# Two token tiles of a gated block computed from centred tokens, with the scale moved into the gelu

## The chip, the cores and the metric

The kernel runs on one core of a Trainium2 chip. The metric is the device time of one execution in microseconds (us); three runs of the kernel before gave a median of 200.08 us. The profile is of one further execution of 199.44 us, whose span from first to last instruction is 197.7 us.

The engines, as the profile names them: PE does the matrix products (PEld is its weight load, which runs beside the products), DVE and ACT do elementwise work, POOL does small work and issues some transfers, and SP only issues transfers. A core has 16 DMA engines that all queues share.

## The reference

`x` is 2048 tokens of 512 channels in bf16. The output is `x + A(xn) + B(xn)`, with `xn` the layer norm of `x`:

```python
def _layernorm(x, axis=-1, eps=1e-05):
    m = mean(x); v = var(x)
    return (x - m) / jnp.sqrt(v + eps)

# A: attention of 32 heads of 16; each query sees 8 keys, 2 apart
qkv = xn @ wqkv
logits = einsum('bhsd,bhswd->bhsw', q, k[idx]) * scale    # idx = pos - {0,2,..,14}
o = einsum('bhsw,bhswd->bhsd', softmax(logits), v[idx])
a = o @ wo

# B: a gated block, F = 1376, half of it 688
z  = gelu(xn @ w_in)
z1 = z[..., :688]
z2 = layernorm(z[..., 688:])
g  = einsum('ts,bsf->btf', w_sp, z2) + b_sp      # mixes all 2048 tokens
b  = (z1 * g) @ w_out

out = x + a + b
```

The norm is a mean to subtract and one factor per token to multiply by. The product with `w_in` is linear in the token, so the factor can be applied before it or after it.

## The kernel before, in words

The tokens are 16 tiles of 128. The program is a set of named steps. Five lists, one for each engine, hold the order in which the engines issue the steps; nothing reorders them, and an instruction that must wait holds all that stands behind it on its engine. The names that matter here, with i the tile:

- `x` loads tokens (tiles 0 to 3 alone, then 4-5, 6-7, 8-11 and 12-15 together) through SP's queue. The same queue carries the weights: `wz0`, `wz1`, `wz2` (the z2 half of `w_in` in three pieces), `wy` (its z1 half), `wk`, `wq`, `wv`.
- `b{i}` and `ag{i}` on DVE make mean and variance of a token (L172 and L178). `gr{i}` on POOL makes the factor: an add of eps (L182; for tiles 0 and 1 an `ep{i}` on DVE, L200, does that) and a power of -1/2 (L183). `n{i}` on DVE writes the normed tile (L186; tile 0 in two halves, L190).
- PE's products need the normed tile turned, with channels on the partitions, in the tile `xnT`. Tiles 0 to 3 are turned by PE itself: `T{i}` is four transposes into PSUM (L225), and `Tc{i}` on ACT copies them to `xnT` (L228; tiles 0, 1 and 2 in two halves). Tiles 4 to 15 are turned by DMA: `t{i}` is a transpose that SP issues (L208). The profile calls the memory of tokens and normed tiles `z`.
- `z{i}` is the z2 half of `xn @ w_in` for a tile: 8 products of 128x344 (L247). Tile 0's are `z0a` and `z0b`; those of tiles 1 and 2 are cut into `Z{i}` (the first few) and `z{i}` (the rest). `h{i}` on ACT is its gelu (L264). `y{i}` and `yg{i}` are the same for the z1 half (L247 and L339).
- `k`, `q`, `v` are the heads (L350), each copied out by ACT (`kc`, `qc`, `vc`, L363). They read `xnT` of all tiles.
- `m`, `f`, `p` on DVE and POOL make the attention logits from q and k in eight units of a quarter of the head's channels and a half of the tokens: `m` multiplies (L393), `f` folds two halves into one by an accumulating DMA that POOL issues (L401; only the first unit's fold is on DVE), `p` sums (L406). `kh` are small copies of k's edges; POOL issues `kh2` and `kh3`.
- `M{j}` mixes all tokens with `w_sp` (L512), and the end of the program multiplies by `wo` and `w_out` (L566, L573, L580), adds and stores.

`wu` is ten products on constants at the very start (L496), and `wd` three more; both only keep PE busy. Three PSUM tiles `mm` go round among z, y, k, q, v and M, two tiles `aux` among the `T`.

The order on PE is `wu T0a T0 B wd z0a T1 z0b Z1 T2 z1 Z2 T3 z2 z3 y0 y1 y2 y3 z4 ... z14`, then the heads, then `z15 y4 ... y15`, `M0 ... M15` and the end.

## Time and profile before

| | before |
|---|---|
| median of three runs | 200.08 us (199.61 to 200.2) |
| the profiled execution | 199.44 us |
| its span | 197.7 us |
| PE busy | 192.8 us, 98% of the span |
| DVE busy | 179.2 us, 91% |
| ACT busy | 87.9 us, 44% |
| POOL busy | 43.4 us, 22% |

A row of a timeline holds the start in us from the span's start, how long the row lasted, the engine (SPq is SP's queue), the line, the operation, out<-in, the shape and how many instructions it merges; in square brackets stand the engine's idle time before it and what ended that. In the view of one line's instructions stand shortest/median/longest in ns, then first and last start in us, and below that the time from a DMA's issue to its landing. A row of the view by stretches holds for each engine its busy time and instruction count, then the granted clock of PE (1.00 is full), the busy share of the DMA engines (it passes 1 when transfers of several queues overlap on an engine) and GB/s. A row of a DMA queue holds packets, MB and the time of the packets as a share of 16 engines over the stretch asked for.

### The profile page before, as it was taken

How to read it: one execution, taken by the hardware profiler on the slowest of the kernel's cores; microseconds unless marked ns; L12 is line 12 of the kernel's file. 1: busy time of each engine (PE TensorE's matmuls, PEld its weight loads, DVE VectorE, ACT ScalarE, POOL GpSimd, SP SyncE). 2: the span in 40 equal slices, each digit the busy share in tenths (PEclk: the TensorE clock that was granted, in tenths of full speed). 3: DMA queues.
4: the chain of work that ended last, by engine and by line, in shares of the span. 5: the costliest groups of instructions: out<-in, count | busy, mean ns of one | idle time of the engine just before them, and what ended most of it. 6: DMA issues, size and time to landing. Idle time of an engine off the chain costs nothing.

```text
span 197.7 us, 4588 instructions
## 1 busy us (share of the span) xinstructions
PE 192.8 (98%) x1944; PEld 121.5 (61%) x1944; DVE 179.2 (91%) x214; ACT 87.9 (44%) x128; POOL 43.4 (22%) x79
## 2 busy tenths in 40 slices
PE   7899999999999999999999999999999999999993
PEld 2466666666666666666666666666666654444442
DVE  4899896799989999999999999999999999999073
ACT  2476798785558967792562311112221110044000
POOL 4477322001565326355000000011120000000000
PEclk9999999999999999999999999999999999999999
DMA  4999552499999999989699999999979227402433
GB/s 148 354 338 133 90 107 83 71 154 135 254 206 211 202 185 146 190 177 185 128 209 252 186 217 276 162 242 266 213 154 241 54 48 219 86 2 83 136 106 106
DMA packets 71252, 33.40 MB, mean 169 GB/s; under 512 B 59488, under 2 KB 69248, under 8 KB 71104
## 3 DMA queue, kind: packets, MB, share of 16 engines
q1 hardware_dynamic: 68400, 25.38, 61.6%
q0 software_dynamic: 2688, 7.70, 20.0%
q8 instruction: 15, 0.25, 0.5%
q10 hardware_dynamic: 144, 0.03, 0.1%
q14 instruction: 5, 0.04, 0.1%
HBM read 10.13 MB, written 2.10 MB: 62 GB/s over the span
## 4 chain that ended last, share of the span: by engine, by line
PE 93%; DMA 2%; SPq 1%; DVE 1%; issue 1%; DVEq 0%
PE mm L512 38%; PE mm L350 21%; PE mm L247 18%; PE mm L580 7%; PE mm L566 6%; PE aux L566 2%; DMA z<-in_A_x_dram 2%; PE mm L573 1%; SPq L255 1%; SPq L165 1%; PE aux L225 0%; DVE stats L172 0%; DVE z L628 0%; DVE z L186 0%; PE aux L580 0%
## 5 line engine op out<-in xcount | busy, mean ns | idle before, releaser
L512 PE MATMUL mm<-z,wsp 128*128 128x344 bf16 x512 | 74.8, 309 | 0.0
L512 PEld LDWEIGHTS <-wsp 128*128 128x128 bf16 x512 | 50.1, 98 | 24.6
L350 PE MATMUL mm<-xnT,wts 128*32 128x512 bf16 x768 | 41.7, 379 | 0.0
L247 PE MATMUL mm<-wts,xnT 128*128 128x344 bf16 x256 | 38.3, 309 | 0.0
L350 PEld LDWEIGHTS <-wts 128*32 128x32 bf16 x768 | 28.7, 139 | 12.8 <-issue 0.3
L460 DVE TENSOR_TENSOR prod<-vp,a_sb 128x4096 bf16<-128x4096 bf16 x16 | 36.2, 2282 | 0.0
L247 PEld LDWEIGHTS <-xnT 128*128 128x128 bf16 x256 | 24.6, 98 | 12.5 <-ACT xnT L228 0.6
L528 ACT ACTIVATE qk<-mm,b_col 128x688 bf16<-128x688 f32 x16 | 13.3, 830 | 42.4 <-PE mm L512 40.2
L393 DVE TENSOR_TENSOR prod<-qk 128x4096 bf16<-128x4096 bf16 (+1 forms) x15 | 27.2, 1860 | 1.2 <-ACT qk L363 1.1
L464 DVE TENSOR_TENSOR prod<-prod,prod 128x8192 bf16<-128x8192 bf16 (+1 forms) x7 | 26.7, 3809 | 0.1
L363 ACT CAST qk<-mm 128x1024 bf16<-128x1024 f32 x16 | 16.2, 1012 | 8.2 <-PE mm L350 8.2
L580 PE MATMUL mm<-wts,xnT 32*128 32x512 bf16 x192 | 14.5, 374 | 0.0
L523 POOL DMA_DIRECT2D qk<-qk x8 | 3.9, 497 | 47.9 <-DMA qk<-z 40.3
L339 ACT ACTIVATE z<-mm 128x688 bf16<-128x688 f32 x16 | 11.8, 742 | 4.2 <-PE mm L247 3.4
L264 ACT ACTIVATE z<-mm 128x688 bf16<-128x688 f32 x16 | 11.8, 744 | 3.2 <-PE mm L247 3.2
L566 PEld LDWEIGHTS <-qk 128*128 128x128 bf16 x75 | 7.3, 98 | 8.9 <-issue 0.4
L566 PE MATMUL mm<-wts,qk 128*128 128x512 bf16 x55 | 12.4, 379 | 0.0
L172 DVE BATCH_NORM_STATS2 stats<-z 128x6 f32<-128x512 bf16 x15 | 10.1, 673 | 2.0 <-DMA z<-in_A_x_dram 1.9
L401 POOL DMA_DIRECT2D prod<-prod x10 | 8.8, 978 | 11.6 <-DVE prod L393 11.6
L580 PEld LDWEIGHTS <-xnT 32*128 32x128 bf16 x256 | 6.7, 93 | 7.2
L183 POOL TENSOR_TENSOR rstd<-rstd,mhalf 128x1 f32<-128x1 f32 x16 | 9.0, 562 | 3.7 <-DVE rstd L200 2.6
L616 ACT CAST z<-mm 128x512 bf16<-128x512 f32 x6 | 3.3, 600 | 13.6 <-PE mm L580 13.6
(93 smaller groups left out, 179.0 us busy)
## 6 DMA issues: line engine op xcount, KB each, us to landing
prod<-prod POOLq DMA_DIRECT2D x10, 512.0 KB, 7.9
wts<-in_A_wo_dram SPq DMA_DIRECT2D x4, 512.0 KB, 6.7
wsp<-in_A_x_dram SPq DMA_DIRECT2D x2, 1024.0 KB, 6.5
out_dram<-z SPq DMA_DIRECT2D x15, 128.0 KB, 1.8
wts<-in_A_wqkv_dram SPq DMA_DIRECT2D x3, 512.0 KB, 6.4
z<-in_A_x_dram SPq DMA_DIRECT2D x2, 512.0 KB, 7.6
wsp<-z POOLq DMA_DIRECT2D x2, 512.0 KB, 8.8
wsp<-wts POOLq DMA_DIRECT2D x2, 512.0 KB, 8.4
```

The costliest lines, as they stand in the source:

```text
L247: PE.matmul(t[:, hh, 0:FHALF], xnT[:, kc, i * P:(i + 1) * P], w_z[part][:, kc, hh * FHALF:(hh + 1) * FHALF], start=(kc == 0), stop=(kc == ...
L264: A.activation(z2[:, i, :].rearrange("p (a b) -> p a b", a=2), t[:, :, 0:FHALF], ACT.Gelu_apprx_tanh, **total)
L339: op_(f"yg{i}", [f"y{i}"] + ["p10"] * (i >= 10), lambda: A.activation(z1u[:, i, 0:FH].rearrange("p (a b) -> p a b", a=2), t[:, :, 0:FHALF] ...
L350: PE.matmul(t[32 * g:32 * g + 32, dd, :], w, r, start=(kc == 0), stop=(kc == C - 1), tile_position=(0, 32 * g))
L363: op_(f"{a}c{p}", [f"{a}{p}"], lambda: A.copy(home(a, p), t[:].rearrange("p d (t s) -> p d t s", t=2)))
L393: V.tensor_tensor(pr[:, w0:w1], q[:, w0:w1], k[:, w0:w1], ALU.mult)
L460: return lambda: V.tensor_tensor(dst, vp[:, :, th, off:off + GS], a_sb[:, th, W - 1 - w].unsqueeze(1).broadcast_to([P, DH, GS]), ALU.mult)
L464: return lambda: V.tensor_tensor(dst, dst, x, ALU.add)
L512: PE.matmul(t[:, hh, 0:FHALF], w[:, k, (j % 2) * P:(j % 2 + 1) * P], z2[:, k, hh * FHALF:(hh + 1) * FHALF], start=(k == 0), stop=(k == NT ...
L528: lambda: A.activation(gs[j % 3].rearrange("p (a b) -> p a b", a=2), t[:, :, 0:FHALF], ACT.Identity, bias=b_col[:, j:j + 1]))
L566: PE.matmul(po[i][:, c], uT[th][:, m, t0:t0 + P], wout[:, m, c], start=(start and m == 0), stop=(stop and m == MF - 1))
L580: PE.matmul(po[groups[n][g]], op[32 * g:32 * g + 32, th, d, s * P:(s + 1) * P], wo_r[32 * g:32 * g + 32, d, :], start=False, stop=(d == DH ...
```

## The change

Four things are changed.

1. **Tiles 0 and 1 are centred, not normed, for z and y.** ACT makes minus the centred tile 0 in two halves (`c0a`, `c0b`, L197), as soon as the mean is there; DVE makes the same of tile 1 (`c1`, L201). PE turns these into `xcT`, a part of the `z2` memory that is free until late in z. The factor is made for both tiles at once on POOL (`gr0`), negated there (`nr`, L202), and taken by the four gelus of these tiles as a scale for each token. The normed tiles 0 and 1 are still made (`n0`, `n1`), since the heads read them; they are now turned by two more DMA transposes, `t0` and `t1`, which SP issues behind `wk` and ahead of `t4`.
2. **The order at the start.** DVE's statistics of tile 2 are one instruction instead of two; eps is added on DVE for tiles 2 and 3 instead of 0 and 1; `n3` stands ahead of `b4`; `wu` has 8 products instead of 10; `B` (which turns the bias) stands behind `T1`; `Z1` and `Z2` have six products each instead of four and two; ACT does `h0` ahead of tile 2's copies.
3. **`y4` and its gelu `yg4` move** from behind the heads to a place right behind `y3`, ahead of `z4`.
4. **`f01`**, the fold of the second unit, moves ahead of `kh2` in POOL's list.

```diff
-    stats2 = sb.tile([P, 2, 6], F32, name="stats2")
+    nrstd = sb.tile([P, 2], F32, name="nrstd")
...
+    xc = [z2_r[:, 13 * FH + n * D:13 * FH + (n + 1) * D] for n in range(2)]
+    xcT = z2_r[:, 13 * FH + 2 * D:13 * FH + 4 * D].rearrange("p (c s) -> p c s", c=C)
...
+    def gscale(i):
+        return {"scale": nrstd[:, i:i + 1]} if i < 2 else {}
...
+    def center_half(n):
         c = slice(n * D // 2, (n + 1) * D // 2)
-        V.tensor_scalar(xn[0][:, c], xs[:, 0, c], mv[:, 0, 0:1], rstd[:, 0:1], ALU.subtract, ALU.mult)
+        A.activation(xc[0][:, c], xs[:, 0, c], ACT.Identity, bias=mv[:, 0, 0:1], scale=-1.0)
+
+    op_("c0a", ["ag0"], lambda: center_half(0))
+    op_("c0b", ["c0a"], lambda: center_half(1))
+    op_("c1", ["ag1"], lambda: V.tensor_scalar(xc[1], xs[:, 1, :], mv[:, 1, 0:1], -1.0, ALU.subtract, ALU.mult))
+    op_("nr", ["gr0"], lambda: G.tensor_scalar(nrstd[:], rstd[:, 0:2], -1.0, 1.0, ALU.mult, ALU.mult))
...
-        if i >= NPE:
+        if tok(i)[1] != "c":
             op_(f"t{i}", [f"n{i}"], lambda i=i: SP.dma_start_transpose(xnT[:, :, i * P:(i + 1) * P], xn[i % 8]))
...
+    def turned_of(i):
+        return xcT[:, :, i * P:(i + 1) * P] if i < 2 else xnT[:, :, i * P:(i + 1) * P]
...
-            PE.matmul(t[:, hh, 0:FHALF], xnT[:, kc, i * P:(i + 1) * P], w_z[part][:, kc, hh * FHALF:(hh + 1) * FHALF],
+            PE.matmul(t[:, hh, 0:FHALF], turned_of(i)[:, kc], w_z[part][:, kc, hh * FHALF:(hh + 1) * FHALF],
                       start=(kc == 0), stop=(kc == C - 1))
...
-    SPLIT = {1: 4, 2: 2}
+    SPLIT = {1: 6, 2: 6}
...
-    op_("wu", [], lambda: spin(aux[1], D, 10))
+    op_("wu", [], lambda: spin(aux[1], D, 8))
...
-    pe = """wu T0a T0 B wd z0a T1 z0b Z1 T2 z1 Z2 T3 z2 z3 y0 y1 y2 y3 z4 z5 z6 z7 z8 z9 z10 z11 z12 z13 z14
+    pe = """wu T0a T0 wd z0a T1 B z0b Z1 T2 z1 Z2 T3 z2 z3 y0 y1 y2 y3 y4 z4 z5 z6 z7 z8 z9 z10 z11 z12 z13 z14
...
-    dve = """b0 ag0 ep0 b1 n0a ag1 ep1 n0 b2a n1 b2 ag2 b3 ag3 n2 b4 ag4 n3 b5 ag5 n4 b6 ag6 n5 b7""".split()
+    dve = """b0 ag0 b1 ag1 c1 b2 ag2 ep2 n0 n2 b3 ag3 ep3 n1 n3 b4 ag4 b5 ag5 n4 b6 ag6 n5 b7""".split()
...
-    pool = ["b16"] + [f"gr{i}" for i in range(NT)] + "zr0 zr4 kh2 f01 f10 zr8 f11 kh3 f20 f21 zr12 f30 f31 LO5 V00 V01 V02 V03".split()
-    sp = """x0 x1 x2 wz0 wz1 wz2 x3 x4 x6 wy x8 x12 wk t4 t5 t6 t7 t8 t9 t10 t11 t12 t13 t14 t15 wq kh0a kh0b W0 kh1 wv W1 vh
+    pool = ["b16"] + ["gr0", "nr"] + [f"gr{i}" for i in range(2, NT)] + "zr0 zr4 f01 kh2 f10 zr8 f11 kh3 f20 f21 zr12 f30 f31 LO5 V00 V01 V02 V03".split()
+    sp = """x0 x1 x2 wz0 wz1 wz2 x3 x4 x6 wy x8 x12 wk t0 t1 t4 t5 t6 t7 t8 t9 t10 t11 t12 t13 t14 t15 wq kh0a kh0b W0 kh1 wv W1 vh
```

How the instructions stand: first SP's queue, where the token loads, `wk` and the transposes of tokens meet. Before:

```order
L259 DMA wts<-in_B_w_in_dram 128x4x688
L165 DMA z_88<-in_A_x_dram 128x4x512 x2
L256 DMA wts<-in_A_wqkv_dram 128x4x512
L208 DMA_TRANSPOSE xnT<-z_88 128x4x128 x12
L257 DMA wts<-in_A_wqkv_dram 128x4x512
```

And now (all lines are about 8 further down in the changed file):

```order
L267 DMA wts<-in_B_w_in_dram 128x4x688
L174 DMA z_88<-in_A_x_dram 128x4x512 x2
L264 DMA wts<-in_A_wqkv_dram 128x4x512
L213 DMA_TRANSPOSE xnT<-z_88 128x4x128 x14
L265 DMA wts<-in_A_wqkv_dram 128x4x512
```

There are 14 transposes instead of 12; the first two are `t0` and `t1`, and `t4` is now the third behind `wk`.

Second, ACT from its start to the gelu of tile 3 (`mm_92` to `mm_94` are the three PSUM tiles of z, `aux_95` and `aux_96` those of the turns). Before:

```order
L659 ACT_TABLE_LOAD
L228 COPY xnT<-aux_95 128x2x128 [waits PE_49]
L228 COPY xnT<-aux_96 128x2x128 [waits PE_49]
L506 CAST b_col<-mm_94 128x16 [waits PE_49]
L228 COPY xnT<-aux_95 128x2x128 [waits PE_49]
L228 COPY xnT<-aux_95 128x2x128
L228 COPY xnT<-aux_96 128x2x128 [waits PE_49]
L228 COPY xnT<-aux_96 128x2x128
L264 ACTIVATE z_86<-mm_92 128x688
L228 COPY xnT<-aux_95 128x4x128 [waits PE_49]
L264 ACTIVATE z_86<-mm_93 128x688
```

And now:

```order
L667 ACT_TABLE_LOAD
L197 ACTIVATE z_86<-z_88,mv 128x256 [waits DMAHW0_49,DVE_49]
L197 ACTIVATE z_86<-z_88,mv 128x256
L236 COPY z_86<-aux_95 128x2x128 [waits PE_49]
L236 COPY z_86<-aux_96 128x2x128 [waits PE_49]
L236 COPY z_86<-aux_95 128x2x128 [waits PE_49]
L236 COPY z_86<-aux_95 128x2x128
L514 CAST b_col<-mm_94 128x16 [waits PE_49]
L272 ACTIVATE z_86<-mm_92,nrstd 128x688 [waits PE_49,Pool_49]
L236 COPY xnT<-aux_96 128x2x128 [waits PE_49]
L236 COPY xnT<-aux_96 128x2x128
L272 ACTIVATE z_86<-mm_93,nrstd 128x688 [waits PE_49]
```

Two activations stand ahead of the first copy, and tile 0's gelu now stands ahead of tile 2's copies and takes `nrstd`, which comes from POOL.

Third, PE at the end of `y3` and the first products of the next tile, which before is `z4`:

```order
L247 LDWEIGHTS xnT
L247 MATMUL mm_93<-wts,xnT 128x344
L247 LDWEIGHTS xnT [waits DMAHW5_49]
L247 MATMUL mm_94<-wts,xnT 128x344 [waits Activation_49]
L247 LDWEIGHTS xnT
```

And now, where it is `y4`:

```order
L255 LDWEIGHTS xnT
L255 MATMUL mm_93<-wts,xnT 128x344
L255 LDWEIGHTS xnT [waits DMAHW7_49]
L255 MATMUL mm_94<-wts,xnT 128x344 [waits Activation_49]
L255 LDWEIGHTS xnT
```

Both wait on the landing of the same transpose, `t4`, at the same place in PE's order, 40 products behind the start of `z3`; it is now on another semaphore, since two more DMAs precede it on SP.

More of the change, by code (lines that the diff above doesn't have):

```diff
@@ L224, in turn @@
         for c in cs:
-            PE.transpose(pt[:, c * P:(c + 1) * P], xn[i % 8][:, c * P:(c + 1) * P], ident[:])
+            PE.transpose(pt[:, c * P:(c + 1) * P], (xc if i < 2 else xn)[i % 8][:, c * P:(c + 1) * P], ident[:])
+    def turned_of(i):
+        return xcT[:, :, i * P:(i + 1) * P] if i < 2 else xnT[:, :, i * P:(i + 1) * P]
     def turned(i, t, c0=0, c1=C):
-        A.copy(xnT[:, c0:c1, i * P:(i + 1) * P], t[:].bitcast(BF16)[:, c0 * P:c1 * P].rearrange("p (c t) -> p c t", c=c1 - c0))
+        A.copy(turned_of(i)[:, c0:c1], t[:].bitcast(BF16)[:, c0 * P:c1 * P].rearrange("p (c t) -> p c t", c=c1 - c0))
     def make_T0():
-        t0 = psum("aux", "T0a", "Tc0a", ["n0a"], lambda t: turn(0, t, (0, 1)))
-        t1 = psum("aux", "T0", "Tc0", ["T0a", "n0"], lambda t: turn(0, t, (2, 3)))
+        t0 = psum("aux", "T0a", "Tc0a", ["c0a"], lambda t: turn(0, t, (0, 1)))
+        t1 = psum("aux", "T0", "Tc0", ["T0a", "c0b"], lambda t: turn(0, t, (2, 3)))
         op_("Tc0a", ["T0a"], lambda: turned(0, t0, 0, 2))
@@ L236, in make_T @@
     def make_T(i):
-        t = psum("aux", f"T{i}", f"Tc{i}", [f"n{i}"], lambda t: turn(i, t))
+        t = psum("aux", f"T{i}", f"Tc{i}", ["c1" if i == 1 else f"n{i}"], lambda t: turn(i, t))
         if i in SPLIT:
```

54 lines of the change are left out of this document (23 added, 31 removed).

## The prediction

> **What bounds the kernel now.** I read the page first, for who is busy; then the chain of work that ended last, for where PE's work becomes unbroken; then PE's waits; then the timeline of the first 20 us and the landings of the DMAs in it.
>
> ```profile
> PE 192.8 (98%) x1944; PEld 121.5 (61%) x1944; DVE 179.2 (91%) x214; ACT 87.9 (44%) x128; POOL 43.4 (22%) x79
> ```
>
> PE is busy for 98% of the span. The chain says more:
>
> ```profile
> 9.87 0.40 PE aux L225 x4
> 10.27 19.54 PE mm L247 x134
> 29.81 41.60 PE mm L350 x768
> ...
> 86.68 74.67 PE mm L512 x512
> ...
> 191.15 2.17 PE aux L566 x10
> ```
>
> From 10.27 us on the chain is PE alone, one stage behind the other, up to the last products near 193.3 us. So DVE's 91% and ACT's 44% set nothing there: whatever is added to or taken from them counts only if it makes PE wait. What can be won lies ahead of 10.9 us, and what can be lost is a new wait of PE anywhere. PE's waits (the line that waited, for whom; us in total, times, longest):
>
> ```profile
> PEld L225 <- DVE z L186: 0.9, 2, 0.5
> PEld L247 <- ACT xnT L228: 0.6, 3, 0.2
> ```
>
> Beside the first turns of tile 0 these are all that the change could remove: 0.9 us for the normed tile ahead of turns, 0.6 us for ACT's copies of turned tiles.
>
> **The start, step by step.** The timeline there, with the sets on which the sum rests:
>
> ```profile
> 0.77 3.90 PE L496 MATMUL aux<-const-bfloat16-1.0 128*128 128x512 bf16 x10 [0.77 <-PEq L718]
> ...
> 3.68 0.18 DVE L178 BATCH_NORM_AGGREGATE mv<-stats 128x2 f32<-128x6 f32 x1
> 5.48 0.37 ACT L228 COPY xnT<-aux 128x256 bf16<-128x256 bf16 x1 [3.47 <-PE aux L225]
> 7.01 1.39 PE L247 MATMUL mm<-wts,xnT 128*128 128x344 bf16 x8
> ...
> 8.51 0.40 PE L225 MATMUL aux<-ident,z 128*128 128x128 bf16 x4
> 8.74 1.09 PE L247 MATMUL mm<-wts,xnT 128*128 128x344 bf16 x6
> 8.94 0.65 ACT L228 COPY xnT<-aux 128x256 bf16<-128x256 bf16 x2 [1.08 <-PE aux L225]
> 9.37 0.11 PEld L247 LDWEIGHTS <-xnT 128*128 128x128 bf16 x2 [0.23 <-ACT xnT L228]
> 9.44 0.38 DVE L186 TENSOR_SCALAR z<-z,mv,rstd 128x512 bf16<-128x512 bf16 x1
> 9.87 0.40 PE L225 MATMUL aux<-ident,z 128*128 128x128 bf16 x4
> 10.31 0.59 ACT L228 COPY xnT<-aux 128x512 bf16<-128x512 bf16 x1
> ...
> 10.94 18.51 PEld L247 LDWEIGHTS <-xnT 128*128 128x128 bf16 x128 [0.16 <-ACT xnT L228]
> ```
>
> `z3` starts at 10.94 (last row), and from there PE loads 128 weights in 18.51 us, 0.145 us each, without a gap. The sum is therefore: when does `z3` start in the changed kernel, and does PE wait later?
>
> The centred halves of tile 0 need only the mean, which is there at 3.86 (3.68 + 0.18), and no power on POOL. The trace has no ACT activation from SBUF of 256 columns; the nearest rows are the copies of 256 columns at 5.48, 0.37 us, and of 512 at 10.31, 0.59 us. I take the first. `c0a` then ends near 4.3 and `c0b`, overlapped as the pair at 8.94 is (0.65 for two), near 4.6; a turn of two blocks (0.3 to its copy) and a copy give the first half of tile 0 at 5.0, against 5.85 (5.48 + 0.37) before. By the second row it would be 5.2. That is 0.6 to 0.8 us won, but the weights are not there:
>
> ```profile
> L255 SPq DMA_DIRECT2D wts<-in_B_w_in_dram x3: 432/434/467, 2.1 to 3.1; - x3
> DMA to landing us min/median/max: 3.7/3.7/3.7
> ```
>
> The three pieces of the z2 weights are issued from 2.1 to 3.1 and land 3.7 us later, at 5.8, 6.3 and 6.8. `z0a` can start at 5.85 at best. Four products of 0.145, `T1` (0.23, from 8.51 to 8.74) and `B` bring `z0b` to 6.7, where its third product meets the last piece at 6.8. Before, it started at 7.01. So 0.3 us is left.
>
> It does not reach `z3`. `z0b` and the six products of `Z1` end at 6.7 + 10 x 0.145 = 8.15. `T2` runs there. `n2`, for which it waited until 8.51, stands ahead of `b3` and `ag3` in DVE's list now, and behind them before, so I take it as done; if it were not, `T2` would stay at 8.51 and everything below come 0.35 us later. From the start of a turn to the start of its copy are 0.43 us (8.51 to 8.94), so the first half of tile 2 is copied from 8.6 to 8.95. The two products left of `z1` end at 8.67 and PE waits 0.3 us. `Z2` starts at 9.0 (before: 9.37), and it now has six products ahead of `T3` instead of two: `T3` starts at 9.0 + 6 x 0.145 = 9.87, exactly where it stood (9.87). `n3`, done at 9.82 before (9.44 + 0.38), has in DVE's list ahead of it one `c1` more (0.4) and `b4` and `ag4` less, and no longer decides. The copy of tile 3 starts 0.44 behind the turn and takes 0.59, so `z3` starts at 9.87 + 0.44 + 0.59 + 0.05 = 10.95 against 10.94. **The start gives nothing**: PE has done more by 9.87, but then waits half a microsecond for a copy that only two products cover. The two spins less cost nothing: ten end at 4.67, eight between 3.9 and 4.3, and the first turn comes at 4.35; the weights at 5.8 cover what might be lost there. Nor do POOL's power over two columns and its negation: they have until `h0`, whose PSUM tile is not wanted again before `z3`.
>
> **What the two new transposes do.** This is where I expect the result. `wk` and the first three transposes of tokens, `t4`, `t5`, `t6`, each with its landing:
>
> ```profile
> L256 SPq DMA_DIRECT2D wts<-in_A_wqkv_dram x1: 1422/1422/1422, 6.7 to 6.7; - x1
> DMA to landing us min/median/max: 8.8/8.8/8.8
> ...
> L208 SPq DMA_TRANSPOSE xnT<-z x1: 1281/1281/1281, 11.0 to 11.0; - x1
> DMA to landing us min/median/max: 5.2/5.2/5.2
> ...
> L208 SPq DMA_TRANSPOSE xnT<-z x1: 1232/1232/1232, 12.4 to 12.4; - x1
> DMA to landing us min/median/max: 4.3/4.3/4.3
> ...
> L208 SPq DMA_TRANSPOSE xnT<-z x1: 1189/1189/1189, 13.8 to 13.8; - x1
> DMA to landing us min/median/max: 4.9/4.9/4.9
> ```
>
> `wk` is issued at 6.7 and lands 8.8 us later, at 15.5. `t4`, issued at 10.97, lands 5.2 us later at 16.17, `t5` (12.4 + 4.3) at 16.7, `t6` (13.8 + 4.9) at 18.7. The first two land half a microsecond apart and right behind `wk`, whenever they were issued: the queue is full and is served in order. The stretches agree (the column ahead of the last is the DMA engines' share, the last GB/s):
>
> ```profile
> 12.00:14.00 2.00, 2.00 (x16) 1.37 (x14) 1.97 (x7) 1.40 (x3) 1.47 (x5) 1.00 1.09 359
> ...
> 17.00:18.00 1.00, 1.00 (x9) 0.66 (x8) 1.00 (x4) 0.74 (x1) 0.78 (x3) 1.00 1.38 16
> ```
>
> From 12 to 14 us the engines are full. Between 17 and 18 they are as full by the share but move 16 GB/s: their packets stand and wait. An answer for the queues from 16.2 to 16.4 names it:
>
> ```profile
> q8 instruction: 1, 0.02, 34.4%
> ```
>
> One packet of instructions, 0.02 MB, took 34.4% of 16 engines x 0.2 us = 1.1 us, on one engine. `t6` was then in work and landed 2 us behind `t5`, though its data take 0.5 us: I read that a transpose is held up as a whole when one of its engines is.
>
> SP has time for the new ones:
>
> ```profile
> 10.97 16.27 SPq L208 DMA_TRANSPOSE xnT<-z  x12
> ```
>
> `wk`'s issue ends at 6.7 + 1.4 = 8.1, SP then issues nothing until 10.97, and a transpose holds it for 1.2 to 1.3 us. `t0` and `t1` wait for `n0` and `n1`, which stand ahead of `n3`, so are done by 9.8; SP is through with both by 11.1 at the latest, and `t4` can be issued as early as before, give or take `n4`, which now stands behind `b5`. The DMA queue is: `t0` and `t1` stand ahead of `t4` behind `wk`. They take the places of `t4` and `t5`, landing at 16.2 and 16.7, and `t4` takes the place of `t6`.
>
> `t4` is read 40 products behind the start of `z3`, by `z4` before and by `y4` now: at 10.94 + 40 x 0.145 = 16.72 before, 0.55 us behind its landing, and at 16.75 now. Moving `y4` shifts no wait there, since it needs the same tile. The bounds for `t4`: 16.7 + 0.5 = 17.2 if nothing holds it up, 18.7 if it meets all that `t6` met. The instruction packet follows PE's progress, I assume; PE has four instructions fewer ahead of it, two weight loads and two products, so it comes 0.3 us later, near 16.65, in the middle of `t4`. Then that engine is free at 17.75 and has about half of its share to do; with the landing I take 18.3, nearest to `t6`'s row. PE then waits from 16.75 to 18.35, and everything behind is late by 18.35 - 16.72 = **1.6 us**.
>
> By the Trainium skill, *DMA: Bandwidth & Descriptors*, section *Queues, rings and completion order*, descriptors on one engine are consumed in ring order and an engine changes between queues only packet by packet; the landings of `wk`, `t4`, `t5` above, in order and half a microsecond apart, agree with the first.
>
> **What lies behind.** The next tiles have room: `z5` comes 16 products, 2.3 us, behind `y4`, and `t5` half a microsecond behind `t4`; `y4` gives every tile from 5 on another 1.17 us. The total of PE's products is unchanged by the move of `y4`, so it costs nothing by itself, but `k` and `q` come 1.17 us later against the rest of PE's program, and with them DVE's logits, which start on a copy of q and later wait 1.25 us for the second fold:
>
> ```profile
> 36.24 4.50 DVE L393 TENSOR_TENSOR prod<-qk 128x4096 bf16<-128x4096 bf16 x2 [1.14 <-ACT qk L363]
> ...
> 59.72 1.23 DVE L406 TENSOR_TENSOR a_sb<-prod 128x2048 bf16<-128x2048 bf16 x1 [1.25 <-DMA prod<-prod]
> ```
>
> The fold goes out ahead of `kh2` now, so I expect this wait to go. That takes back the 1.17 us. At the end DVE must be in time for PE's last stages (two quarters of the head output, which PE starts at 178.14 and 182.03):
>
> ```profile
> 175.38 1.22 DVE L468 TENSOR_TENSOR xnT<-prod 128x2048 bf16<-128x2048 bf16 x1
> ...
> 178.14 3.62 PE L580 MATMUL mm<-wts,xnT 32*128 32x512 bf16 x64
> 178.91 1.22 DVE L468 TENSOR_TENSOR xnT<-prod 128x2048 bf16<-128x2048 bf16 x1
> ...
> 182.03 0.37 PE L580 MATMUL mm<-wts,xnT 32*128 32x512 bf16 x1
> ```
>
> DVE is done at 176.60 and 180.13, 1.5 and 1.9 us ahead. Even if the fold gains nothing, 1.17 us fits in. So the fold and `y4` come to nothing either way. ACT's scale by token is one operand more on the same instruction and hidden in its 56% of idle time.
>
> **Sum.** 0 for the start, +1.6 for the wait on `t4`, 0 for the rest: 199.44 + 1.6 = 201.0 for an execution like the profiled one. That execution is 0.64 below the median of 200.08, on which the forecast stands: 201.7.
>
> **Rivals.**
>
> *The transpose is late but not held up.* If the instruction packet misses `t4`, it lands at 17.2 and PE loses 0.5 us: 200.6. For it: the packet need only come 0.3 us later than I think, or wait with PE itself. Against it: 1.1 us of packet starting anywhere from 16.0 to 16.9 meets `t1` or `t4`. The Trainium skill, *Runtime: NRT & Kernel Launch*, section *Instruction fetch mechanics*, says that instructions come in blocks of 16 KiB by the sequencer's own queue and that the cost is mostly hidden; by that the result would be this one, and `t6`'s landing above speaks against it.
>
> *Not slower: `t4` is in time.* If the two new transposes slip into gaps of the queue instead of standing ahead of `t4`, it lands by 16.7, PE does not wait, and the time is 200.0, with the 0.3 us at `Z2` perhaps on top (199.8). The point that decides is a landing of `t4` at or before 16.72. The full engines from 12 to 14 us and `wk`'s 8.8 us speak against it.
>
> *More is late.* If `t5` or a later tile meets the packet as well, if PE falls back to the slow pace that its first spins show, or if DVE's logits slip by more than 1.5 us, another microsecond is lost: 202.7 or more. The room of 2.3 us at `z5` speaks against the first; no row of this trace shows PE idle for 1.6 us, so the second is open.
>
> **How the numbers follow.** Held up: 0.58. Late but not held up: 0.20. In time: 0.14. More late: 0.08. The first spreads by the packet's place, a landing from 18.0 to 18.7, so 201.4 to 202.1. The range is to leave out no more than 2 in 10: from 200.2, which takes in the unhindered landing and the upper edge of the case in time (0.11 of it lies below), to 202.5, beyond which lies most of the worst case (0.07). About 0.3%, 0.6 us, is what a measurement of this kernel can tell from no change. The held-up case and the worse one are slower by more (0.66), and a third of the unhindered one (0.07); the rest of that one and most of the case in time are within it (0.22); 0.05 of the case in time is left for faster, which needs twice what the start could give.
>
> **What would show it.** PE's weight load for `y4` should wait about 1.6 us on a DMA that writes `xnT`, near 16.8; `z3` should start at 10.9 to 11.0; `t0` and `t1` should land near 16.2 and 16.7, `t4` near 18.3; DVE should not wait for the second fold; the last stages should be as unbroken as before. I am wrong if `z3` starts 0.3 us or more earlier, or if `t4` lands by 16.7.

## The result and the profile after

The changed kernel takes 201.56 us (median of six runs, 201.32 to 201.80) beside 200.14 us of the kernel before on the same chip (six runs, 199.61 to 200.62). The ratio is 1.0073, 95% interval 1.0056 to 1.0091: slower by 1.4 us. The forecast was 201.7.

The profiled execution took 201.55 us, with a span of 199.7 us. That is 2.1 us more than the profiled execution before, while the medians differ by 1.4; the difference is taken up below.

The busy times of the page, and the chain of work that ended last (start, duration, what):

```profile
PE 192.7 (96%) x1942; PEld 120.9 (61%) x1942; DVE 179.6 (90%) x213; ACT 89.3 (45%) x130; POOL 45.2 (23%) x78
```

```profile
13.02 5.94 DMA xnT<-z
19.00 14.17 PE mm L255 x96
33.18 41.60 PE mm L358 x768
74.78 14.11 PE mm L255 x96
88.88 74.67 PE mm L520 x512
```

PE's work is the same, 192.7 us; its share fell from 98% to 96%. PE's unbroken stretch begins at 19.00 now, and what the chain shows ahead of it is a transpose by DMA, issued at 13.02 and landed at 18.96: `t4`. `M0` (L520) starts at 88.88 instead of 86.68, so 2.2 us were lost by then, and 2.0 are left at the end of the span.

PE's first products of z in the timeline of the changed kernel, with its waits in brackets:

```profile
5.73 0.74 PE L255 MATMUL mm<-wts,z 128*128 128x344 bf16 x4 [0.46 <-DMA wts<-in_B_w_in_dram]
...
6.74 1.63 PE L255 MATMUL mm<-wts,z 128*128 128x344 bf16 x10
8.21 0.39 PE L230 MATMUL aux<-ident,z 128*128 128x128 bf16 x4
...
9.06 1.05 PE L255 MATMUL mm<-wts,xnT 128*128 128x344 bf16 x6 [0.17 <-ACT xnT L236]
9.95 0.39 PE L230 MATMUL aux<-ident,z 128*128 128x128 bf16 x4
...
11.01 1.34 PE L255 MATMUL mm<-wts,xnT 128*128 128x344 bf16 x8 [0.39 <-ACT xnT L236]
...
19.00 14.17 PE L255 MATMUL mm<-wts,xnT 128*128 128x344 bf16 x96 [1.99 <-DMA xnT<-z]
```

The rows are, in order, `z0a`, `z0b` with `Z1`, `T2`, `Z2`, `T3`, `z3` and `y4`. `z3` starts at 11.01, against 10.94 before: the start gave nothing. `y4` starts at 19.00, after 2 us of idle time. PE's waits as a whole (in us, times, longest):

```profile
PEld L255 <- DMA xnT<-z: 2.3, 1, 2.3
PEld L255 <- ACT xnT L236: 1.3, 2, 0.7
...
PEld L588 <- DVE xnT L476: 0.3, 1, 0.3
```

The weight load waited 2.3 us, the products behind it 2.0, since some of theirs were still in work. The third row is new too, and lies at the end; it is taken up with the fold.

The first turn by DMA, `t0`, and later `t4`, in the view of their line (duration of the issue, start, then issue to landing):

```profile
L213 SPq DMA_TRANSPOSE xnT<-z x1: 3762/3762/3762, 7.8 to 7.8; - x1
DMA to landing us min/median/max: 8.6/8.6/8.6
...
L213 SPq DMA_TRANSPOSE xnT<-z x1: 1830/1830/1830, 13.0 to 13.0; - x1
DMA to landing us min/median/max: 5.9/5.9/5.9
```

`t0` lands at 16.46 and `t1` at 16.94, in the places that `t4` and `t5` had. Then nothing lands for two microseconds, until `t4` at 18.96. In between, from 16.6 to 17.0, the view of the DMA queues has one packet of instructions:

```profile
q8 instruction: 1, 0.02, 17.8%
```

17.8% of 16 engines over 0.4 us are 1.14 us on one engine; the packet starts at 16.73.

### The profile page after: what moved, and what is told of

It is laid out like the page before. It is cut to its first block, busy times and chain, and to the rows that moved or that the text cites. A ratio compares the mean times of both kernels' runs of the same rounds, so it can differ in the third digit from the quotient of the medians.

```text
span 199.7 us, 4591 instructions
## 1 busy us (share of the span) xinstructions
PE 192.7 (96%) x1942; PEld 120.9 (61%) x1942; DVE 179.6 (90%) x213; ACT 89.3 (45%) x130; POOL 45.2 (23%) x78
## 4 chain that ended last, share of the span: by engine, by line
PE 88%; DMA 5%; DVE 2%; SPq 1%; POOL 1%; issue 1%; DVEq 0%
PE mm L520 37%; PE mm L358 21%; PE mm L255 14%; PE mm L588 7%; PE mm L574 6%; DMA xnT<-z 3%; PE aux L574 2%; DMA z<-in_A_x_dram 2%; DVE stats L181 1%; PE mm L581 1%; SPq L263 1%; SPq L174 1%; POOL rstd L189 1%; DVE z L192 1%; DVE z L636 0%
## 5 line engine op out<-in xcount | busy, mean ns | idle before, releaser
L520 PE MATMUL mm<-z,wsp 128*128 128x344 bf16 x512 | 74.8, 309 | 0.0
L520 PEld LDWEIGHTS <-wsp 128*128 128x128 bf16 x512 | 50.1, 98 | 24.6
L358 PEld LDWEIGHTS <-wts 128*32 128x32 bf16 x768 | 28.2, 139 | 13.3 <-issue 0.3
L255 PE MATMUL mm<-wts,xnT 128*128 128x344 bf16 x224 | 33.7, 309 | 2.5 <-DMA xnT<-z 2.0
L255 PEld LDWEIGHTS <-xnT 128*128 128x128 bf16 x224 | 21.5, 98 | 14.3 <-DMA xnT<-z 2.3
L409 POOL DMA_DIRECT2D prod<-prod x10 | 9.4, 1050 | 25.2 <-DVE prod L401 25.1
L347 ACT ACTIVATE z<-mm 128x688 bf16<-128x688 f32 x14 | 10.3, 738 | 5.5 <-PE mm L255 5.0
L181 DVE BATCH_NORM_STATS2 stats<-z 128x6 f32<-128x512 bf16 x16 | 10.8, 672 | 1.8 <-DMA z<-in_A_x_dram 1.7
L272 ACT ACTIVATE z<-mm 128x688 bf16<-128x688 f32 x14 | 10.4, 741 | 3.8 <-PE mm L255 3.8
L189 POOL TENSOR_TENSOR rstd<-rstd,mhalf 128x1 f32<-128x1 f32 (+1 forms) x15 | 8.7, 582 | 2.8 <-DVE rstd L204 1.7
```

The lines of the kernel that those rows point to most:

```text
L181: V.bn_stats(stats[:, i, :], xs[:, i, :])
L189: G.tensor_tensor(rstd[:, i:i + n], rstd[:, i:i + n], mhalf[:, 0:n], ALU.pow)
L255: PE.matmul(t[:, hh, 0:FHALF], turned_of(i)[:, kc], w_z[part][:, kc, hh * FHALF:(hh + 1) * FHALF], start=(kc == 0), stop=(kc == C - 1))
L358: PE.matmul(t[32 * g:32 * g + 32, dd, :], w, r, start=(kc == 0), stop=(kc == C - 1), tile_position=(0, 32 * g))
L520: PE.matmul(t[:, hh, 0:FHALF], w[:, k, (j % 2) * P:(j % 2 + 1) * P], z2[:, k, hh * FHALF:(hh + 1) * FHALF], start=(k == 0), stop=(k == NT ...
```

## The experiments

The theory is that of the prediction: two more transposes stand ahead of `t4` in a full queue, a packet of instructions then holds `t4`, and `y4` waits; nothing else of the change moves the time. Eleven kernels test its parts; one of them was run twice.

### The place in the queue: wk behind t7

```diff
-    sp = """... x8 x12 wk t0 t1 t4 t5 t6 t7 t8 ...
+    sp = """... x8 x12 t0 t1 t4 t5 t6 t7 wk t8 ...
```

> The load of wk is issued behind t7 instead of ahead of t0; nothing else changes. Theory (t4 is late because of its place in a full queue, and because an instruction packet stands between t1 and t4): the transposes follow the last tokens, t4 lands near 15.6 us, ahead of the packet, y4 does not wait, and the time falls by the whole wait of 2.0 to 2.2 us, to 199.4 to 199.6. Rival (a third transpose in a row always lands 2 us behind the second): t4 near 17.1, a wait of 0.3 us, 199.8. Rival (the loss is not in the order of the queue): 201.5 as with the change.

200.88 us, ratio 1.0057 (1.0035 to 1.0079); the profiled execution took 200.65. The wait for `t4` is gone, and another has come. PE's weight loads in the timeline:

```profile
14.59 8.12 PEld L255 LDWEIGHTS <-xnT 128*128 128x128 bf16 x56
23.99 0.99 PEld L255 LDWEIGHTS <-xnT 128*128 128x128 bf16 x8 [1.28 <-DMA xnT<-z]
```

The first row runs through `y4` without a break: `t4` landed at 15.92 (15.6 expected), right behind `t1` (15.45), so a third transpose in a row is not late as such. The second row is `z8`, which waits 1.28 us for `t8`. `t8` landed at 23.95; it now stands behind `wk` (landed at 22.66). An 8 KB packet of instructions starts at 22.21, so how much of the 1.29 us between the two landings is the packet's is not shown. The time, 199.4 to 199.6 expected, missed by 1.3 us: I had looked only at `t4` and not at which tile the moved load would be in front of. PE's products stood still for 0.93 us there, and `z3` started at 11.22, 0.28 behind the profile of before; together these are the 1.2 us by which the profiled execution is longer.

### The two turns alone: the kernel before with two more transposes

```diff
+    xd = z2_r[:, 13 * FH:13 * FH + 2 * D].rearrange("p (c s) -> p c s", c=C)
...
+    for i in range(2):
+        op_(f"d{i}", [f"n{i}"], lambda i=i: SP.dma_start_transpose(xd[:, :, i * P:(i + 1) * P], xn[i]))
...
-    sp = """... x8 x12 wk t4 t5 ...
+    sp = """... x8 x12 wk d0 d1 t4 t5 ...
```

> The kernel before with nothing added but two DMA transposes ahead of t4, of the normed tiles 0 and 1 into memory that is free then; nobody reads them. Theory (the place in the queue and the packet are the whole of the loss): t4 takes the place that t6 had, lands at 18.6 to 18.9, z4 waits 1.9 to 2.2 us, and the time is 202.0 to 202.3. Rival (the centring, the order at the start or y4 make the loss): t4 lands by 17.2 and the time is 200.1 to 200.6.

201.57 us, ratio 1.0088 (1.0066 to 1.0109). Here `y4` is not ahead, so the wait stands at `z4`:

```profile
19.07 5.95 PEld L251 LDWEIGHTS <-xnT 128*128 128x128 bf16 x42 [2.06 <-DMA xnT<-z]
```

`t4` landed at 19.03 and `z4` waited 2.06 us, both as expected (the landing 0.1 later). Two transposes that nobody reads, put into the kernel before, make the whole loss of the change: the ratio is 1.0088 against 1.0073, and the intervals overlap. The time lies 0.4 us below the expected range, which was built on the 200.1 of before; beside these runs before took 199.85 us.

### The packet: five products on constants less

```diff
-    op_("wu", [], lambda: spin(aux[1], D, 8))
-    op_("wd", ["T0"], lambda: spin(mm[1][:, 0, :], P, 3))
+    op_("wu", [], lambda: spin(aux[1], D, 6))
```

> The changed kernel with five products on constants less (wu has 6, wd is gone), so PE comes to its next block of instructions ten instructions, 0.7 us, later. Theory (the packet of instructions holds the transpose that is next): the packet starts near 17.4 instead of 16.7, t4 lands at 17.4 to 17.5 ahead of it, y4 waits 0.6 to 0.7 us instead of 2, and the time is 200.0 to 200.2. Rival (a third transpose in a row always lands 2 us behind the second, whatever the packet does): t4 near 18.9 and 201.5. A start that is later by some tenths, from a colder PE, would be seen at z3.

201.07 us, ratio 1.0070 (1.0049 to 1.0090). The packet moved further than I meant, to 18.76, since PE itself was 1.2 us late (`z3` at 12.21). The view of the queues from 18.6 to 19.0 us:

```profile
q8 instruction: 1, 0.02, 26.4%
```

and PE's weight loads:

```profile
15.58 9.43 PEld L255 LDWEIGHTS <-xnT 128*128 128x128 bf16 x65
```

With the packet out of the way, `t0`, `t1` and `t4` landed at 16.66, 17.14 and 17.63, half a microsecond apart, and `y4` (within the row of 65 loads) did not wait. The next transpose that met the packet was `t7`: `t6` landed at 18.84, `t7` at 22.08. So it is the packet that makes the gap. The time hardly fell (200.0 to 200.2 were expected), since the wait was exchanged for the later start (PE's slow pace, told below), and the weight load of `z14` waited 0.6 us for `t14`, which another packet held.

The same gap stands in the other traces. Start and duration of a packet, and the landing of the transpose that it held (one that lands within 0.25 us of the packet's start still passes):

| kernel | packet: start, duration | transpose | landed | behind the packet's start |
|---|---|---|---|---|
| before | 16.38, 1.10 | t6 | 18.67 | 2.29 |
| before | 20.56, 0.62 | t10 | 22.58 | 2.02 |
| changed | 16.73, 1.14 | t4 | 18.96 | 2.23 |
| changed | 21.92, 0.72 | t9 | 24.12 | 2.20 |
| wk behind t7 | 15.77, 1.38 | t5 | 18.08 | 2.31 |
| two turns | 16.81, 1.13 | t4 | 19.03 | 2.22 |
| five less | 18.76, 1.69 | t7 | 22.08 | 3.32 |
| y4 back, second (below) | 30.98, 0.64 | t15 | 32.24 | 1.26 |
| the two turns last (below) | 28.88, 0.51 | t15 | 30.32 | 1.44 |

The last two rows show that the distance from the packet's start is not a fixed cost. There the queue is not full; the held transposes landed 3.1 to 3.2 us behind their issue, where their neighbours take 2.3 to 2.5.

The single packets of the trace show where a hold ends. In the changed kernel 29 packets of SP's queue began between 17.22 and 17.59 us and all ended between 18.66 and 18.71, 0.8 us behind the end of the packet of instructions (17.87). In the kernel before, 25 of them ended between 18.34 and 18.39, 0.9 us behind its end (17.48). Behind the second packet of each trace it is 0.7 us. Other packets of a transpose last 0.02 to 0.06 us. So the transpose is held as a whole, and for longer than the packet of instructions lasts.

### The move of y4, undone

```diff
-    pe = """... y0 y1 y2 y3 y4 z4 z5 ...  z15 y5 ...
+    pe = """... y0 y1 y2 y3 z4 z5 ...  z15 y4 y5 ...
```

(and `yg4` likewise on ACT)

> The changed kernel with y4 and yg4 back behind the heads. Theory (the move of y4 is worth nothing by itself, since z4 needs the same tile): z4 waits 2.0 to 2.3 us for t4 in y4's place, and the time is that of the changed kernel, 201.4 to 201.7. Rival (the 1.17 us by which k and q come later costs or wins something): another time by 0.3 us or more, 201.2 or less if the move costs.

> The kernel of e2 once more, for the cause of its spread: its profiled run took 201.32 us and three others 202.39 to 203.13. Theory (y4 ahead gives every tile behind it 1.17 us of room, and without it a held transpose makes PE wait a second time): an execution of 202.3 us or more shows a second wait on a DMA that writes the turned tokens, 0.8 to 2 us, at one of z8 to z10 or at k0, which t15 reached only 0.8 us ahead in the profile of e2. Rival (the spread comes from the end): no second wait there, but one of PE on DVE near 178 to 183 us. An execution of 201.3 us shows neither and leaves it open.

The first gave 202.44 us (201.32 to 203.13), ratio 1.0129 (1.0091 to 1.0168): slower than the changed kernel by 0.9 us by the medians and 1.1 by the ratios. Its profiled execution, of 201.32 us, was the fastest of the four and shows the wait at `z4` alone, of 2.38 us. The repetition, a single run, took 201.77 us. The chain of the one, then of the other, from `z4` on:

```profile
18.84 13.01 PE mm L255 x88
31.85 41.60 PE mm L358 x768
```

```profile
19.11 13.01 PE mm L255 x88
32.12 41.77 PE mm L358 x768
```

In the second a packet at 30.98 us held `t15`, which landed at 32.24, behind the start of `k0` at 32.12; the heads took 41.77 us instead of 41.60. In the first `t15` had landed at 31.02. So the last tile can come too late for `k0` when `y4` stands behind the heads. In the changed kernel `k0` starts 1.2 us later against the tiles (33.18, with `t15` at 31.26). Whether this makes the executions of 202.4 to 203.1 us long is not shown: none of them was profiled, and the one case seen cost 0.2 us. For the longest there is another candidate. Its mean granted clock was 0.992, as in the execution of 203.03 us of the next experiment, and 0.997 to 1.00 in all others on record; 0.8% of PE's 192.7 us are 1.5 us by estimate. The two of 202.39 and 202.49 us stay open.

### The fold, undone

```diff
-    pool = ... zr4 f01 kh2 f10 ...
+    pool = ... zr4 kh2 f01 f10 ...
```

> The changed kernel with f01 back behind kh2 in POOL's list. DVE's p01 waits again, 1 to 1.3 us, so DVE's work behind it is 3.4 us later than in the kernel before where it is 2.2 later now. Theory (DVE's lateness counts only where PE reads the head output at the end, where some 1.5 us of room were left and 1.4 are used now): the wait of PE on DVE there grows from 0.3 us to between 0.3 and 1.3, and the time is 201.6 to 202.5. Rival of the prediction's own step (the fold and the move of y4 are worth nothing either way): 201.4 to 201.7 and no longer wait at the end.

201.53 us (201.25 to 203.03), ratio 1.0103 (1.0071 to 1.0135), the interval wide for one run at 203.03. The median is that of the changed kernel. DVE's `p01`:

```profile
61.54 1.22 DVE L414 TENSOR_TENSOR a_sb<-prod 128x2048 bf16<-128x2048 bf16 x1
```

There is no wait ahead of it, though the fold stands behind `kh2` as before. So, by this one execution, that order does not decide the wait, and my theory of the end falls with it: PE did not wait there at all, as the rival said. In the changed kernel the fold is issued at 51.36 us, 1.8 us sooner than in this one, and the same step still waits 0.28. How long the accumulating transfers take varies by more than that: the seven of that stretch took between 6.5 and 10.3 us to land before, the six here between 5.8 and 9.9.

DVE's side of the end in the changed kernel, and PE's weight load there:

```profile
39.62 4.50 DVE L401 TENSOR_TENSOR prod<-qk 128x4096 bf16<-128x4096 bf16 x2 [3.27 <-ACT qk L371]
...
61.90 1.23 DVE L414 TENSOR_TENSOR a_sb<-prod 128x2048 bf16<-128x2048 bf16 x1 [0.28 <-DMA prod<-prod]
...
98.20 1.23 DVE L416 TENSOR_TENSOR prod<-prod 128x2048 bf16<-128x2048 bf16 x1 [0.62 <-DMA wts<-in_B_w_out_dram]
...
178.99 1.22 DVE L476 TENSOR_TENSOR xnT<-prod 128x2048 bf16<-128x2048 bf16 x1
```

```profile
180.27 3.20 PEld L588 LDWEIGHTS <-xnT 32*128 32x128 bf16 x64 [0.26 <-DVE xnT L476]
```

Against before, DVE is 3.4 us later at the first row, 2.2 at the second, 3.6 at the third and fourth. PE is 2.2 us later, so DVE lost 1.4 of the 1.5 us that it had in hand. The weight load waited 0.26 us; the loads behind it took 3.20 us instead of 3.35, and the next group starts at 184.01 against 181.81 before, 2.2 later as at `M0`. So this wait cost nothing, but the room is used up.

### The two turns last

```diff
+    xm = [prod[1][:, n * D:(n + 1) * D] for n in range(2)]
...
-    V.tensor_scalar(xn[i % 8], ...
+    V.tensor_scalar(xm[i] if i < 2 else xn[i % 8], ...
...
-    sp = """... wk t0 t1 t4 t5 ... t14 t15 wq ...
+    sp = """... wk t4 t5 ... t14 t15 t0 t1 wq ...
```

> The changed kernel with t0 and t1 at the end of the transposes, behind t15; n0 and n1 are written to memory of their own, so that n8 and n9 need not wait for t0 and t1. Theory (the place in the queue is the whole loss, and the start gives nothing): t4 lands at 16.1 to 16.6, y4 does not wait, z3 starts at 10.8 to 11.3, and the time is that of the kernel before, 199.7 to 200.2; k0 may have to wait up to 0.5 us for t1, which would make it 200.6. Rival (centring wins time at the start, and the wait hid it): 199.5 or less. Rival (the end, where DVE is later against PE by the move of y4, costs by itself): 200.5 and a wait of PE on DVE at the end.

201.05 us, ratio 1.0067 (1.0052 to 1.0083). No tile of z or y waits; `t4` landed at 16.61. But the heads do:

```profile
32.44 3.90 PE L360 MATMUL mm<-xnT,wts 128*32 128x512 bf16 x68 [1.22 <-DMA xnT<-prod]
```

`t1` landed at 32.31, and `k0`, which reads all tiles, began at 32.44. I had allowed 0.5 us for this and it was 1.2. SP issues a transpose every 1.31 us here, so two more behind the twelve come 2.6 us later; the twelve were themselves 1.2 us later than before (`t15` issued at 27.20, 26.02 before). Before, `t15` landed at 28.46 and `k0` began at 29.81, so there were 1.35 us in hand; `k0` itself would have come at 31.22 here, 1.4 us later. A packet (28.88) held `t15` to 30.32, but `t1` landed 2.5 us behind its issue, so that hold cost at most 0.2 us here. The rival that the centring wins at the start is not borne out: `z3` began at 11.21. Nor is that of the end: PE does not wait for DVE there.

### `wk` on ACT's queue, and a shorter start

The last five kernels try to let `t0` and `t1` stand where SP has time for them, with no load of `wk` ahead, and all but one to shorten the start by `Z2` of three products. The first:

```diff
-    SPLIT = {1: 6, 2: 6}
+    SPLIT = {1: 6, 2: 3}
...
-    op_("wk", [], lambda: SP.dma_start(w_k, wq_d[:, :, D:2 * D]))
+    op_("wk", ["yg4"], lambda: A.dma_start(w_k, wq_d[:, :, D:2 * D]))
...
-    act = """... yg3 yg4 h4 ...
+    act = """... yg3 yg4 wk h4 ...
-    sp = """... x8 x12 wk t0 t1 ...
+    sp = """... x8 x12 t0 t1 ...
```

> The changed kernel with wk issued by ACT behind yg4 instead of by SP ahead of t0, so that all transposes follow the last tokens, and with Z2 of three products ahead of T3 instead of six. Theory: t4 lands near 15.9, ahead of y4 or held by the packet to no later than y4; T3 is no longer behind six products and z3 starts at 10.6 to 10.8 where the last tokens land as in the profile of before, 0.3 us sooner than before; no tile waits; 199.5 to 200.0 beside 199.9 to 200.1 of before. Rival (the packet holds t4 or t5 and the transfer of wk beside the transposes delays a later tile): a wait of 0.5 to 1.5 us on a DMA, 200.5 to 201.5.

200.03 us (eleven runs), ratio 1.0008 (0.9996 to 1.0019): not to be told from before. PE's weight loads for `z3` and `z8`, then the load of `wk`:

```profile
10.66 0.99 PEld L255 LDWEIGHTS <-xnT 128*128 128x128 bf16 x8 [0.30 <-ACT xnT L236]
...
23.38 7.99 PEld L255 LDWEIGHTS <-xnT 128*128 128x128 bf16 x56 [1.19 <-DMA xnT<-z]
```

```profile
L264 ACTq DMA_DIRECT2D wts<-in_A_wqkv_dram x1: 476/476/476, 18.7 to 18.7; - x1
...
DMA to landing us min/median/max: 4.4/4.4/4.4
```

`z3` starts 0.3 us sooner than before, and `t4` (16.14) is in time. `wk` came through another queue, from 18.7 to 23.04, and `t8` landed 0.3 us behind it, at 23.34, where `t7` had landed at 19.27, although `t8` had been issued first (18.24 against 18.68). The single packets show that SP's queue stood meanwhile: `wk`'s 528 packets began between 19.95 and 22.58, and of SP's none between 20.09 and 21.80. The 512 packets with `t8`'s data had all begun by 20.09; of the packets of 4 B that close each transpose none began before 21.80. The wait of 1.19 us at `z8` eats the gain.

The next kernel issues the same load behind `h8`, at 23.9 us, and the one after it has `Z2` of six products again:

```diff
-    act = """... yg4 wk h4 h5 h6 h7 h8 sq8 ...
+    act = """... yg4 h4 h5 h6 h7 h8 wk sq8 ...
```

```diff
-    SPLIT = {1: 6, 2: 3}
+    SPLIT = {1: 6, 2: 6}
```

> The kernel of e8 with wk issued behind h8 instead of behind yg4, some 6 us later. In e8 the data of wk moved from 21 to 23 us, t8 landed at 23.34, and z8 waited 1.19 us. Theory (that wait was the collision with wk, and by 25 us the transposes have 1.5 to 2 us of room): t8 lands at 20.5 to 22, no tile waits, wk lands at 28 to 30, ahead of k0 near 30.5, and the time is 1.2 us below that of e8: 198.6 to 199.0, faster than before by 0.9 to 1.3 us. Rival (a packet of instructions near 22 us holds t8 or t9 anyway): a wait of 0.5 to 1.2 us stays, 199.3 to 200.0.

> The kernel of e9 with Z2 of six products ahead of T3 as in the change. Theory (the six products make T3 and its copy late, and that is all of what the centring won): z3 starts at 10.9 to 11.2 instead of 10.6 to 10.8, and the time is 0.3 us above that of e9. Rival (z3 is late for n3 and not for the order): the same z3 and the same time within 0.1 us.

The first took 200.49 us, ratio 1.0033 (1.0020 to 1.0046), where 198.6 to 199.0 were expected. Its profiled execution, the fastest, took 199.69 us and shows the collision moved with the load:

```profile
28.86 2.15 PEld L255 LDWEIGHTS <-xnT 128*128 128x128 bf16 x16 [0.69 <-DMA xnT<-z]
```

`wk` landed at 28.41, `t13` at 28.82, `z13` waited 0.69 us. `wk` set `t13` back by some 2.2 us (it landed 3.5 us behind `t12` where its neighbours are 1.3 apart), and the room of `z13` took 1.5 of them, not all as I had thought. The median lies another 0.8 us above this execution; what the other five lost there is open.

The second took 200.84 us (199.74 to 201.71), ratio 1.0038 (1.0019 to 1.0057). Its runs lie in two groups, four from 199.74 to 199.95 and eight from 200.55 to 201.71, and its profiled execution is of the second. There PE ran `z0a`, `z0b` and `Z1` at a slow pace:

```profile
6.09 1.30 PE L255 MATMUL mm<-wts,z 128*128 128x344 bf16 x4 [0.56 <-DMA wts<-in_B_w_in_dram]
...
7.88 2.34 PE L255 MATMUL mm<-wts,z 128*128 128x344 bf16 x10
```

against 0.74 and 1.63 us in the changed kernel's profile. `z3` starts at 12.85. The two orders of `Z2` can therefore not be compared by these medians. By the profiles, `z3` starts 1.94 to 1.95 us behind the start of `Z2` with six products (the changed kernel, the two turns last, this one) and 1.51 to 1.64 with three (the two kernels ahead of it and the two below): the six cost 0.3 to 0.4 us, but no time shows it.

The last two cut `wk` in four, issued by ACT behind `h5` to `h8`, once with ten products in `wu` and one in `wd` (the last lines of the diff), once with eight and three.

```diff
+    for n in range(4):
+        op_(f"wk{n}", [f"h{n + 5}"], lambda n=n: A.dma_start(w_k[:, n:n + 1, :], wq_d[:, n:n + 1, D:2 * D]))
...
-    act = """... h4 h5 h6 h7 h8 sq8 ...
+    act = """... h4 h5 wk0 h6 wk1 h7 wk2 h8 wk3 sq8 ...
...
-    op_("wu", [], lambda: spin(aux[1], D, 8))
-    op_("wd", ["T0"], lambda: spin(mm[1][:, 0, :], P, 3))
+    op_("wu", [], lambda: spin(aux[1], D, 10))
+    op_("wd", ["T0"], lambda: spin(mm[1][:, 0, :], P, 1))
```

> The changed kernel with Z2 of three products, with wk in four loads of 128 KB that ACT issues behind h5, h6, h7 and h8, and with ten products on constants in wu as before (wd has one, so that PE's count of instructions is that of the change). Theory (a load delays the transposes behind it by its own transfer, 2.5 to 3 us for the whole of wk in e8 and e9, so 0.6 to 0.8 us for a quarter, which the transposes catch up; and ten spins leave PE at its fast pace, which eight do not always do): z0a takes 0.74 us for four products, z3 starts at 10.6 to 10.9, no tile waits more than 0.3 us, and the time is 198.7 to 199.3, faster than before by 0.6 to 1.2. Rival (a packet holds one of t8 to t15 beside the loads): a wait of 0.5 to 1.2 us on a DMA, 199.5 to 200.2.

> The kernel of e11 with wu and wd as in the change, eight and three. Theory (two spins less leave PE at its slow pace for 0.5 us in most executions and for several us in some, and here no wait for t4 hides it): z0a takes 1.0 to 1.3 us, the runs spread over 1 us or more, as in e10 (199.74 to 201.71), and the median is 0.2 to 1.0 us above that of e11. Rival (the pace at the start costs nothing, for the weights set it): the median of e11 within 0.15 us and a spread below 0.8.

201.29 us, ratio 1.0070 (1.0048 to 1.0091), and 201.57 us, ratio 1.0078 (1.0052 to 1.0104). The first expectation missed by 2 us. In the second the distance from the first kernel (0.28 us) and the spread (1.8 us) came out, but not their reason: `z0a` took 0.74 us, not 1.0 to 1.3. ACT in the timeline of the second:

```profile
23.35 0.38 ACTq L265 DMA_DIRECT2D wts<-in_A_wqkv_dram  x1
23.77 0.74 ACT L273 ACTIVATE z<-mm 128x688 bf16<-128x688 f32 x1 [2.81 <-PE mm L255]
```

ACT was through with `h5` at 20.96 and could issue `wk0` only at 23.35, right behind the landing of `t9` at 23.32, which a packet (21.41) had held. In the trace the transfers of SP's and ACT's queues take eight completion counters in turn, and each issue waits for the landing of the transfer that had its counter before it; `wk0` got that of `t9`, `wk1` that of `t10`, `wk2` that of `t11`, and each was issued 0.02 to 0.03 us behind that landing. So ACT waited for a held transpose that has nothing to do with `wk`, and with it the gelu behind it and then PE, which needed the gelu's PSUM tile: 0.9, 0.5 and 0.3 us. The first of the two has in addition a wait at the end:

```profile
179.81 3.14 PEld L589 LDWEIGHTS <-xnT 32*128 32x128 bf16 x64 [1.15 <-DVE xnT L477]
```

There DVE was late beyond the room it has. The question of the spins stays open: `z0a` took 0.96 us with ten of them and 0.74 with eight, in one execution each. No version was faster than the kernel before.

## Why the prediction was right

**The start.** Each step came within 0.12 us: `z0a` at 5.73 (5.85), `z0b` at 6.74 (6.7), `T2` at 8.21 (8.15), `Z2` at 9.06 (9.0), `T3` at 9.95 (9.87), `z3` at 11.01 (10.95). One term was mis-sized without effect: the two halves `c0a` and `c0b` took 0.91 us together where I took 0.65 from the copies, but the weights set `z0a`. That two spins less cost nothing held in this profile; the runs with late starts show that it need not hold in each execution. In the changed kernel `y4` waits for the queue anyway, and up to 2 us of a late start vanish in that wait.

**The queue.** `t0`, `t1` and `t4` took the places forecast (16.46, 16.94, and `t6`'s for `t4`), the packet came at 16.73 (16.65), and `y4` waited. The sizes were off: `t4` landed at 18.96 instead of 18.3, and `y4` was late by 2.2 us instead of 1.6. The step that failed is "that engine is free at 17.75 and has about half of its share to do". The packet of instructions did end near that time (17.87), but the held packets of `t4` on SP's queue ended only at 18.66 to 18.71, and `t4` landed 0.3 us behind them. Why the hold lasts 0.8 us longer than the packet is not shown. The bound of 18.7, taken from `t6`'s landing, was 0.3 too low; `t6`'s distance from its packet, 2.29 us, would have given 19.0.

A second step failed and cost nothing here: "SP is through with both by 11.1 at the latest, and `t4` can be issued as early as before". The issue of `t0` lasted 3.76 us, where I took 1.2 to 1.3, and `t4` was issued at 13.02 instead of 10.97. Where the queue is not full, a transpose lands 2.4 us behind its issue, which would be 15.4 and so ahead of `t1`'s landing (16.94): the place in the queue set the landing and not the issue. But all tiles come later by it; `t15` landed at 31.26 instead of 28.46, in time only because `k0` was 3.4 us later too.

**The forecast of the median.** I put the 1.6 us on the median by adding the 0.64 us by which the profile of before lies below it. The changed kernel's profile lies on its median (201.55 and 201.56), so this term was wrong by 0.6 us, in the other direction than the wait, and the two errors cancel: that 201.7 came so near to 201.56 is luck. A reason lies near: before, a late start makes a late end; in the changed kernel the wait takes it up. In five executions with that wait (the changed kernel, y4 back twice, the fold back, the two turns) `z3` starts at 11.01, 10.81, 10.81, 10.89 and 11.35, and the product that waits at 19.00, 18.84, 19.11, 18.77 and 19.07, spread over 0.34 instead of 0.54 us and in another order. The times agree with it: the six runs of before spread over 1.0 us, the six of the changed kernel over 0.5. That this is all of the 0.6 us is argued, not shown.

**y4 and the fold.** "It costs nothing by itself" fits the two profiled executions with `y4` back, 201.32 and 201.77 us beside 201.55. Their kernel's median is 0.9 us above the changed kernel's, by three executions that were not profiled; whether the move wins something is open. That the wait for the second fold goes because the fold goes out ahead of `kh2` was wrong; 0.28 us of it are left, and without the move it is gone as well. The margins at the end, 1.5 and 1.9 us, held, but 1.4 us of the first are used, more than the 1.17 that I counted at the most.

**The rivals.** Late but not held up (17.2) and in time (16.7) are both excluded by the landing at 18.96. Of more being late, `t9` met a second packet and landed at 24.12, but in time. What the Trainium skill says in *Runtime: NRT & Kernel Launch*, section *Instruction fetch mechanics*, that crossing a block costs little that is not hidden, does not hold here for others than the engine that fetches: a transpose that was next in line, and whose reader had no room, made PE wait 2 us.

## What to carry to other kernels

Before a transfer is added to a full queue, write down for each transfer behind it when it lands and when its reader needs it; the smallest difference, here 0.55 us at tile 4, is the room, and what the addition delays beyond it, the reader waits. Moving the load instead moved the wait here to `z8` and `z13`. A DMA that is next in line in a full queue when an engine fetches instructions landed here some 2 us behind that packet's start, so a margin below that is one that a change in the number of instructions can use up. Where the profile before has such a margin and a start that varies, compare the change with the profiled execution and with the median separately: a new wait can swallow the variation and make the medians differ by less than the profiles.

## What the hardware showed that was not expected

- A packet of instructions of 8 or 16 KB on one DMA engine holds a whole transpose of 128x512, and longer than it lasts itself: the held packets ended 0.7 to 0.9 us behind its end in the profiles of before and after. With the 16 KB packets, which met the full queue, the held transpose landed 1.9 to 2.3 us behind the packet's start in twelve of the fourteen profiles (3.3 with a packet of 1.69 us; in the kernel with ten spins, where two transposes still landed behind the packet's start, the third came 2.9 us behind it). With two 8 KB packets near 30 us it was 1.3 and 1.4 us. Otherwise such transposes land 0.5 us apart when the queue is full.
- A load of 512 KB on ACT's queue stops the transposes on SP's: while it ran, no packet of SP's queue began for 1.7 us (`wk` behind `yg4`) and 2.5 us (`wk` behind `h8`). `t8` landed 0.3 us and `t13` 0.4 us behind `wk`, 4.1 and 3.5 us behind the transpose ahead of them.
- PE's pace at the start differs between executions of nearly the same program. With the same eight and three spins ahead, the four products of `z0a` took 0.74 us in six profiled executions (the changed kernel and five experiments), 1.03 to 1.26 in three and 1.30 in one; the column of the granted clock shows 1.00 for all of them. The Trainium skill, *TensorE: Matmul & The Clock Gate*, section *Part 1: The HAM clock gate (the "warmup" mystery)*, says that the fast pace comes after some 3.4 us of activity in a window that does not start with the kernel, so that the number of slow products varies from run to run; the rows agree with that, and a cover of spins that just suffices in one profile is not a safe one.
